# Top-k attention and a leaky-ReLU MLP on one core: eight pairs of q and k on chip, and the first two chunks' MLP work begun a step later

## The chip, the cores and the metric

The kernel runs on one core of a Trainium2 chip. The metric is device time in microseconds (us) of one execution; five executions were timed. One more was recorded by the hardware profiler, and all durations below come from that one. The engines are called by the profile's names: PE is TensorE (matrix products), DVE is VectorE, ACT is ScalarE, POOL is GpSimd, SP is SyncE, whose queue issues all DMA transfers here. Each engine, and SP's queue, works through its own list of instructions in order. The simple arrow `out<-in` in the profile names the tile written and the tiles read.

## The reference: what is computed

For 8 batches and 8 heads, with 576 tokens and a head dimension of 64, all in float32:

```python
scores = scale * np.matmul(q, k.transpose(0, 1, 3, 2))
kth = np.partition(scores, -top_k, axis=-1)[..., -top_k:-top_k + 1]   # top_k = 32
scores = np.where(scores >= kth, scores, -1000000000.0)
attn = np.exp(scores - np.max(scores, axis=-1, keepdims=True))
attn = attn / (np.sum(attn, axis=-1, keepdims=True) + 1e-09)
a = np.matmul(attn, v)
x = a.transpose(0, 2, 1, 3).reshape(4608, 512)
h = x @ w_in                                                          # 512 x 2048
out = np.maximum(0.01 * h, h) @ w_out                                 # 2048 x 512
```

The two weight matrices come as float64 words and are rounded to float32 on the chip.

## The kernel before, in words

**Weights first.** Sixteen pieces of 1 MB are loaded into `raw` tiles (three buffers, L61 and L101), and each is rounded by `round_weights` (L104 to L149) with ACT, DVE, POOL and PE. ACT and POOL read the `raw` tile; after the last piece the three `raw` buffers lie idle.

**Pairs and units.** Two heads form a pair, so a batch has four pairs and there are 32 in all. Pair p's q and k are loaded by `load_qk` (L155) into tiles `qt` and `kt` with `LOADED = 5` buffers each (L56, L60), its v by `load_v` (L162), also five. The attention works on 144 units. A whole unit is 128 query rows of one pair (both heads); a left unit is 64 rows of two pairs. An even batch has its two left units last, an odd batch has them first, so at the beginning of an odd batch all four of its pairs are needed at once (L185 to L191).

**Steps.** The main loop (L503) has one step s for each unit, written out by hand; the order of the calls is the order of the instructions on every engine. In step s:

- `top_k` of unit s runs on DVE in four parts (four calls of `slot`): one max and one min pass (L240), then MAX8 and MATCH_REPLACE8 rounds.
- `mask` of unit s-1 on POOL (L258, L259), `exponents` of it on ACT (L262), and `sums` (L267), which writes `ze`.
- `reciprocals` of unit s-2 on DVE (L271), behind the first part of `top_k(s)`: it waits for `ze`. Then `normalize` on ACT (L274).
- The normalized weights of unit s-2 are transposed: usually by `transpose` (L276), with two `split` copies on ACT (L283), two DMAs to DRAM (`apart`, L284) and a DMA transpose into `wT` (L286). For the units 3, 7, 15, 23 and 31 (`HURRIED`) it is `transpose_in_haste` on PE (L296) with two copies by ACT (L302).
- In an even step, `scores` (L193) of units s+2 and s+3: PE writes two `wide` and one `narrow` PSUM tile (L210), ACT copies them out (L217).
- `values(s)` (L491): PE multiplies `wT` by v into a `wide` PSUM tile (L323), and ACT copies the result into `x`, the input of the MLP (L337). Before step `HURRY = 20` the scores stand ahead of the values, after it behind them.
- `load_more(s)` (L464) ends the step: it loads another pair's q and k if the buffers allow, which is when the pair five places earlier has had its last scores.

**The MLP** works on chunks of tokens: two of 128, then 17 of 256 (L53). A chunk is ready when the values of its last units are there (`attended`): chunk 0 in step 5, chunk 1 in step 9, chunk 2 in step 17. Its work is a generator that yields after each small piece with that piece's cost in PE columns (`mlp`, and `hidden_of_few` for the first two chunks, `EARLY = 2`). `mlp_steps(budget)` takes pieces while the budget owed is positive; it is called seven times in each step: five times among the parts of the step above, and twice behind `values`, at its end. Until chunk 2 is ready the budget of a call is 530, later it is the backlog spread over the calls until the next chunk (`slot_budget`). When nothing is ready, what is owed is set to zero.

A piece of the first two chunks is two matmuls of 512 columns (L348 into `ph`, or L386 into `pz`) or four transposes (L358). Behind the pieces stand ACT's Prelu into `scale` (L353), ACT's copy of the transposes into `gT` (L359), and at the chunk's end ACT's copy `o_sb` (L393) and the output's DMA on SP (L394). From chunk 2 on, L374 and L380 take the place of L348 to L359. The `ph`, `pt` and `pz` tiles share two PSUM buffers.

Of the kernel before, what the change touches and what calls it, by code (L numbers as in the profile page):

```python
# [8 lines left out]
F32 = mybir.dt.float32  # L9
U32 = mybir.dt.uint32  # L10
U16 = mybir.dt.uint16
# [8 lines left out]
def kernel(  # L20
# [14 lines left out]
    NPAIR, P, S = qT.shape  # L35
# [14 lines left out]
    WCH = 1024  # L50
# [5 lines left out]
    LOADED, LOADED_V = 5, 5  # L56
# [3 lines left out]
    loads = ctx.enter_context(tc.tile_pool(name="loads", bufs=LOADED))  # L60
    raws = ctx.enter_context(tc.tile_pool(name="raws", bufs=3))  # L61
# [33 lines left out]
    def load_weights(n):  # L95
        if n >= NPIECE:
            return
        if not AS_WORDS:
            nc.sync.dma_start(piece(n), weights[n])
            return  # L100
        raw_of[n] = raws.tile([P, WCH, 4], U16, name="raw")  # L101
        nc.sync.dma_start(raw_of[n].rearrange("p n w -> p (n w)"), weights[n])
# [50 lines left out]
    qk_of, v_of = {}, {}  # L153

    def load_qk(pi):  # L155
        qt = loads.tile([P, S], F32, name="qt")
        kt = loads.tile([P, S], F32, name="kt")
        nc.sync.dma_start(qt, qT[pi])
        nc.sync.dma_start(kt, kT[pi])
        qk_of[pi] = qt, kt  # L160

    def load_v(pi):  # L162
        v_of[pi] = loads.tile([P, NKC, 2, D], F32, name="vt", bufs=LOADED_V)
        nc.sync.dma_start(v_of[pi], vk[pi])
# [54 lines left out]
    def first_scores(u):  # L219

        ps = [ps_sc.tile([P, 2, 512], F32, name="wide", bufs=2) for i in range(2)]
        for half in range(2):
            for i, pi, side, r0 in u.parts:
                qt, kt = qk_of[pi]
                d = slice(side * D, (side + 1) * D)
                nc.tensor.matmul(ps[i][:, half, 0:HS], qt[d, u.q0:u.q0 + P],
                                 kt[d, half * HS:(half + 1) * HS], start=True, stop=True)
        u.both = work.tile([P, 2, S], F32, name="s_sb", bufs=5)
        u.s = [u.both[:, i, :] for i in range(2)]
        for i in range(2):  # L230
            nc.scalar.copy(u.s[i].rearrange("p (h n) -> p h n", h=2), ps[i][:, :, 0:HS])
# [107 lines left out]
    EARLY = 2  # L339
# [22 lines left out]
    def mlp(ch):  # L362

        n = CHUNKS[ch]
        t0 = sum(CHUNKS[:ch])
        x = x_of[ch]
        if ch < EARLY:
            yield from hidden_of_few(x)
        for f0 in range(0, NFC if ch >= EARLY else 0, 2):
            ph = ps_ml.tile([P, 2, CHMAX], F32, name="ph", tag="ml")  # L370
            for i in range(2):
                f = f0 + i
                for c in range(HP):
                    nc.tensor.matmul(  # L374
                        ph[:, i, 0:n], w_in[c][:, f * P:(f + 1) * P], x[c][:, 0:n],
                        start=(c == 0), stop=(c == HP - 1),
                    )
                    if c == 1 or i == 0 and c == HP - 1:
                        yield 2 * max(n, 225)
            nc.scalar.activation(gT[:, f0:f0 + 2, 0:n], ph[:, :, 0:n], AF.Prelu, alpha=SLOPE)  # L380
            yield 2 * max(n, 225)
        for r0 in range(0, n, P):
            m = min(P, n - r0)
            pz = ps_ml.tile([P, 512], F32, name="pz", tag="ml")
            for f in range(NFC):
                nc.tensor.matmul(  # L386
                    pz[0:m, 0:DMODEL], gT[:, f, r0:r0 + m], w_out[f // 4][:, f % 4, :],
                    start=(f == 0), stop=(f == NFC - 1),
                )
                if f % 2 and f + 1 < NFC:  # L390
                    yield 2 * DMODEL
            o_sb = work.tile([P, DMODEL], F32, name="o_sb", bufs=1)
            nc.scalar.copy(o_sb[0:m], pz[0:m, 0:DMODEL])  # L393
            nc.sync.dma_start(out[t0 + r0:t0 + r0 + m, :], o_sb[0:m])  # L394
            yield 2 * DMODEL
# [10 lines left out]
    def mlp_steps(budget):  # L406
        owed[0] += budget
        while owed[0] > 0:
            if running[0] is None:
                if not ready:  # L410
                    owed[0] = 0.0
                    return
                running[0] = mlp(ready.pop(0))
            cost = next(running[0], None)
            if cost is None:
                running[0] = None
            else:
                owed[0] -= cost
                backlog[0] -= cost
# [2 lines left out]

    LAG = 3
    HURRY = 20
    HURRIED = {3, 7, 15, 23, 31}

    def values_at(n):

        return n + LAG + (n + LAG) % 2 - ((n | 1) in HURRIED)

# [13 lines left out]
    def attended(s):  # L444
        for at, ch in ready_at:
            if at == s:
                ready.append(ch)
                backlog[0] += mlp_cost(ch)

    def slot_budget(s):  # L450

        after = [at for at, _ in ready_at if at >= s]
        until = after[0] if after else s
        if len(after) >= len(CHUNKS) - EARLY:
            return EARLY_SHARE
        return backlog[0] / ((until + 1 - s) * SLOTS)
# [4 lines left out]
    with tc.manual_schedule():  # L461
        last = {p: n for n, u in enumerate(steps) for p in u.pairs}

        def load_more(s):  # L464

            for of, load, n, lag in ((qk_of, load_qk, LOADED, -2), (v_of, load_v, LOADED_V, LAG + 1)):
                while len(of) < NPAIR and (len(of) < n or last[len(of) - n] + lag <= s):
                    load(len(of))


        for n in range(3):
            load_weights(n)
        rounding = {}
        for n in range(NPIECE + 2):
            for i in (n, n - 1, n - 2) if AS_WORDS else ():
                if 0 <= i < NPIECE:
                    if i == n:
                        rounding[i] = round_weights(i)
                    next(rounding[i], None)
            load_weights(n + 3)  # L480
            if 6 <= n < 6 + HP:
                load_qk(n - 6)
            elif n == NPIECE - 3:
                first_scores(steps[0])
            elif n == NPIECE:
                first_scores(steps[1])
            if n == NPIECE - 1:
                load_v(0)
                load_v(1)

        def values(s):  # L491
            due = [u for n, u in enumerate(steps) if values_at(n) == s]
            if due:
                po = ps_sc.tile([P, 2, 512], F32, name="wide", bufs=2)[:, 0, 0:2 * P]
                po = po.rearrange("p (u n) -> p u n", u=2)
            else:
                return
            for part in (weigh_values, keep_values):
                for n, u in enumerate(due):
                    part(u, po[:, n, :])  # L500
            attended(s)

        for s in range(len(steps) + LAG + 1):  # L503
            cur, old, older, new = unit(s), unit(s - 1), unit(s - 2), ()
            if s % 2 == 0:
                new = [u for u in steps[s + 2:s + 4] if u]
            picks = top_k(cur) if cur else iter(())
            budget = slot_budget(s)

            def slot():  # L510
                next(picks, None)

            slot()
            if old:
                mask(old, 0)
                mask(old, 1)
            if older:
                reciprocals(older)
                normalize(older, 0)
                normalize(older, 1)  # L520
            mlp_steps(budget)
            slot()
            if s - 2 in HURRIED:
                transpose_in_haste(older)
            mlp_steps(budget)
            if old:
                exponents(old, 0)
            if older:
                keep_transposed(older) if s - 2 in HURRIED else transpose(older)
            slot()  # L530
            mlp_steps(budget)
            mlp_steps(budget)
            slot()
            mlp_steps(budget)
            if old:
                exponents(old, 1)
                sums(old)
            if new and s < HURRY:
                scores(new)
            values(s)  # L540
            if new and s >= HURRY:
                scores(new)
            budget = slot_budget(s + 1)
            mlp_steps(budget)
            mlp_steps(budget)
            load_more(s)
        mlp_steps(1e9)

# [57 lines left out]
```

## Time and profile before

| | |
|---|---|
| five timed executions, median | 1491.41 us (1488.08 to 1496.42) |
| the profiled execution's own time | 1491.77 us |
| its span, first to last instruction | 1490.0 us |
| mean granted clock of PE | 0.979 of full |
| longest waits of PE between 100 and 250 us | 15.0 us for ACT's score copies, 13.0 us for k |
| first matmul of chunk 2 (L374) | 242.72 us |
| DVE's start of step 17 | 225.74 us |

In the profile's groups a line gives the source line, the engine, the operation, the tile written and read, the shape, the count, the busy time and the mean of one; in an order of time, the start, the length, the instruction, and in brackets how long the engine was idle before it and what ended that wait. Each 512-column float32 matmul of the program stands as two records in the order of time.

### The profile page before, as it was taken

What the parts mean: (1) busy time and instruction counts of PE and PEld (TensorE: products, weight loads), DVE (VectorE), ACT (ScalarE), POOL (GpSimd) and SP (SyncE); (2) the same over time, 40 slices, a digit from 0 to 9 for tenths busy, and PEclk for the clock granted to TensorE, in tenths of its full rate; (3) what the DMA queues carried; (4) which work ended last, traced back from release to release, by engine and by line L of the source; (5) the groups of instructions that cost most, each with busy time, mean ns of one, the idle gap of its engine ahead of it and who ended that gap; (6) DMA issues with size and microseconds to landing.
All of it is one profiled execution on the core that took longest, in us unless ns stands there. A gap on an engine that the chain in (4) does not pass through costs nothing.

```text
span 1490.0 us, 24127 instructions
## 1 busy us (share of the span) xinstructions
PE 1400.8 (94%) x8077; PEld 932.3 (63%) x8077; DVE 1328.6 (89%) x3414; ACT 1095.5 (74%) x1979; POOL 1096.0 (74%) x742
## 2 busy tenths in 40 slices
PE   6708987999999999999999999999999999999998
PEld 2305546676666766676766666767676767676674
DVE  7999998999999999999999999999999999999600
ACT  8647786777788877777777777777777777777720
POOL 2277787888788887788887887888888887788700
PEclk9968998999999999999999999999999999999999
DMA  8623354535566466555664556656755465645510
GB/s 323 252 64 85 99 166 128 164 110 148 153 168 160 137 161 173 169 136 159 174 176 126 137 165 174 165 142 151 182 161 144 129 169 147 169 128 142 144 46 14
DMA packets 386172, 221.12 MB, mean 148 GB/s; under 512 B 331520, under 2 KB 331520, under 8 KB 384000
## 3 DMA queue, kind: packets, MB, share of 16 engines
q1 hardware_dynamic: 386048, 219.59, 53.0%
q8 instruction: 63, 1.03, 0.3%
q14 instruction: 61, 0.50, 0.1%
HBM read 46.14 MB, written 91.42 MB: 92 GB/s over the span
## 4 chain that ended last, share of the span: by engine, by line
PE 84%; DVE 6%; ACT 4%; DMA 4%; issue 1%; SPq 0%; POOL 0%; DVEq 0%; ACTq 0%
PE pz L386 34%; PE ph L374 28%; PE wide L323 11%; PE wide L210 6%; PE narrow L210 3%; DMA wT<-apart 2%; ACT split L283 2%; DMA apart<-split 1%; DVE tops L245 1%; ACT s_sb L274 1%; DVE pairs L248 1%; ACT s_sb L262 1%; PE ph L348 1%; DVE w_out L149 1%; DVE w_in L149 1%
## 5 line engine op out<-in xcount | busy, mean ns | idle before, releaser
L258 POOL TENSOR_SCALAR pen<-s_sb,tops 128x576 f32<-128x576 f32 x288 | 637.4, 2213 | 224.6 <-DVE tops L245 136.6
L245 DVE MAX8 tops<-pairs 128x8 f32<-128x288 f32 (+1 forms) x1152 | 636.0, 591 | 0.0
L386 PE MATMUL pz<-w_out,gT 128*128 128x512 f32 x1152 | 508.3, 596 | 1.4 <-ACT gT L359 1.4
L374 PE MATMUL ph<-x,w_in 128*128 128x256 f32 x2176 | 481.1, 381 | 0.0
L248 DVE MATCH_REPLACE8 pairs<-tops,pairs 128x288 f32<-128x288 f32 (+1 forms) x864 | 460.2, 538 | 0.0
L374 PEld LDWEIGHTS ph<-x,w_in 128*128 128x128 f32 x2176 | 410.7, 190 | 77.1 <-issue 22.9
L259 POOL TENSOR_TENSOR s_sb<-s_sb,pen 128x576 f32<-128x576 f32 x288 | 406.2, 1410 | 24.1
L386 PEld LDWEIGHTS pz<-w_out,gT 128*128 128x128 f32 x1152 | 215.3, 190 | 266.1 <-issue 263.4
L283 ACT COPY split<-s_sb 128x1152 uint16<-128x1152 uint16 x278 | 304.8, 1145 | 0.0
L262 ACT ACTIVATE s_sb<-s_sb,nbias 128x576 f32<-128x576 f32 x288 | 221.1, 768 | 12.4 <-POOL s_sb L259 12.4
L274 ACT ACTIVATE s_sb<-s_sb,rz 128x576 f32<-128x576 f32 x288 | 207.1, 770 | 25.6 <-DVE rz L271 25.6
L240 DVE TENSOR_TENSOR pairs<-s_sb 128x576 f32<-128x576 f32 x288 | 213.4, 779 | 9.9
L323 PEld LDWEIGHTS wide<-wT,vt 128*64 128x64 f32 x3200 | 162.6, 140 | 65.9 <-issue 18.5
L323 PE MATMUL wide<-wT,vt 128*64 128x128 f32 (+1 forms) x3200 | 181.3, 270 | 23.2 <-ACT s_sb L217 15.0
L210 PE MATMUL wide<-kt,qt 64*128 64x352 f32 (+1 forms) x632 | 118.4, 488 | 27.2 <-ACT s_sb L217 22.0
L337 ACT COPY x<-wide 128x128 f32<-128x128 f32 (+1 forms) x160 | 32.2, 261 | 151.4 <-PE wide L323 151.4
L380 ACT ACTIVATE gT<-ph 128x512 f32<-128x512 f32 x136 | 80.6, 593 | 78.9 <-PE ph L374 78.9
L217 ACT COPY s_sb<-wide 128x704 f32<-128x704 f32 x142 | 107.1, 754 | 21.7 <-PE wide L210 21.7
L210 PE MATMUL narrow<-kt,qt 64*128 64x224 f32 (+1 forms) x632 | 69.9, 359 | 8.5 <-DMA kt<-in_kT_dram 8.5
L210 PEld LDWEIGHTS wide<-kt,qt 64*128 64x128 f32 (+1 forms) x632 | 48.8, 178 | 44.4 <-ACT s_sb L217 22.5
L271 DVE RECIPROCAL rz<-ze 128x2 f32<-128x2 f32 x144 | 22.4, 156 | 59.9 <-ACT ze L267 59.8
L217 ACT COPY s_sb<-narrow 128x448 f32<-128x448 f32 x142 | 68.6, 536 | 6.8 <-PE narrow L210 6.1
(58 smaller groups left out, 550.3 us busy)
## 6 DMA issues: line engine op xcount, KB each, us to landing
apart<-split SPq DMA_DIRECT2D x278, 288.0 KB, 2.1
raw<-in_weights_dram SPq DMA_DIRECT2D x16, 1024.0 KB, 6.3
vt<-in_vk_dram SPq DMA_DIRECT2D x32, 320.0 KB, 3.4
qt<-in_qT_dram SPq DMA_DIRECT2D x32, 288.0 KB, 3.5
kt<-in_kT_dram SPq DMA_DIRECT2D x32, 288.0 KB, 4.0
out_dram<-o_sb SPq DMA_DIRECT2D x36, 256.0 KB, 2.0
wT<-apart SPq DMA_TRANSPOSE x139, 4.6
```

The lines of the kernel that those rows point to most:

```text
L210: nc.tensor.matmul(to[r0:r0 + u.rows, i, :], qt[d, u.q0:u.q0 + u.rows], kt[d, k0:k1], start=True, stop=True)
L240: nc.vector.tensor_tensor(pairs[:, :, n, :], u.both[:, :, 0:HS], u.both[:, :, HS:S], op)
L245: nc.vector.max(out=u.tops[:, i, r, :], in_=rest[i])
L248: nc.vector.match_replace(out=rest[i], in_to_replace=u.tops[:, i, r, :], in_values=rest[i], imm_value=LOWEST)
L258: nc.gpsimd.tensor_scalar(pen, u.s[i], u.tops[:, i, ROUNDS - 1, 7:8], MASKED, ALU.is_lt, ALU.mult)
L259: nc.gpsimd.tensor_tensor(u.s[i], u.s[i], pen, ALU.add)
L262: nc.scalar.activation(u.s[i], u.s[i], AF.Exp, bias=u.nbias[:, i:i + 1], scale=SCALE, accum_out=u.z[:, i:i + 1])
L274: nc.scalar.activation(u.s[i], u.s[i], AF.Copy, bias=0.0, scale=u.rz[:, i:i + 1])
L283: nc.scalar.copy(split, pairs[:, :, h])
L323: nc.tensor.matmul(po[side * D:(side + 1) * D, o, :], vt[:, c, side, :], u.wT[:, c + side * NKC if c + 1 < NKC else c, r:r + n], start=(c ...
L374: nc.tensor.matmul(ph[:, i, 0:n], w_in[c][:, f * P:(f + 1) * P], x[c][:, 0:n], start=(c == 0), stop=(c == HP - 1),)
L386: nc.tensor.matmul(pz[0:m, 0:DMODEL], gT[:, f, r0:r0 + m], w_out[f // 4][:, f % 4, :], start=(f == 0), stop=(f == NFC - 1),)
```

## The change

`load_qk` uses eight places in turn for the pairs. Five are the tiles of before; the pairs 5 to 7 of every eight go into `raw` tiles, with q in the first 576 words of a partition and k in the next 576. `load_more` therefore keeps eight pairs instead of five. The first call of it, at the end of step 0, now loads pairs 4 to 7 where it loaded pair 4; these loads stand ahead of those of v for pairs 2 to 4. `HURRIED` becomes a tuple, and in the steps 5 and 9, which end with the last values of chunks 0 and 1, the two calls of `mlp_steps` behind the values are left out. The budget of the other calls stays as it was.

```diff
     def load_qk(pi):
-        qt = loads.tile([P, S], F32, name="qt")
-        kt = loads.tile([P, S], F32, name="kt")
+        if pi % (LOADED + 3) < LOADED:
+            qt = loads.tile([P, S], F32, name="qt")
+            kt = loads.tile([P, S], F32, name="kt")
+        else:
+            raw = raws.tile([P, WCH, 4], U16, name="raw").rearrange("p n w -> p (n w)").bitcast(F32)
+            qt, kt = raw[:, 0:S], raw[:, S:2 * S]
         nc.sync.dma_start(qt, qT[pi])
         nc.sync.dma_start(kt, kT[pi])
         qk_of[pi] = qt, kt
...
-    HURRIED = {3, 7, 15, 23, 31}
+    HURRIED = (3, 7, 15, 23, 31)
...
-            for of, load, n, lag in ((qk_of, load_qk, LOADED, -2), (v_of, load_v, LOADED_V, LAG + 1)):
+            for of, load, n, lag in ((qk_of, load_qk, LOADED + 3, -2), (v_of, load_v, LOADED_V, LAG + 1)):
                 while len(of) < NPAIR and (len(of) < n or last[len(of) - n] + lag <= s):
                     load(len(of))
...
-            budget = slot_budget(s + 1)
-            mlp_steps(budget)
-            mlp_steps(budget)
+            if s - 2 not in HURRIED[:EARLY]:
+                budget = slot_budget(s + 1)
+                mlp_steps(budget)
+                mlp_steps(budget)
             load_more(s)
```

## The prediction

> **What bounds the kernel now.** I read the page first, then the waits and the busy windows by stage, then the order of time on TensorE (PE), ScalarE (ACT) and the DMA queue (SP) around the last long wait. The page's share of busy time and its chain by engine:
>
> ```profile
> PE 1400.8 (94%) x8077; PEld 932.3 (63%) x8077; DVE 1328.6 (89%) x3414; ACT 1095.5 (74%) x1979; POOL 1096.0 (74%) x742
> ...
> PE 84%; DVE 6%; ACT 4%; DMA 4%; issue 1%; SPq 0%; POOL 0%; DVEq 0%; ACTq 0%
> ```
>
> PE holds the end, but not everywhere. What PE waited for between 100 and 250 us, and then after 250:
>
> ```profile
> PE wide L323 <- ACT s_sb L217: 15.0, 2, 14.1
> PE narrow L210 <- DMA kt<-in_kT_dram: 8.5, 2, 8.3
> PE wide L210 <- DMA kt<-in_kT_dram: 4.5, 1, 4.5
> ```
>
> ```profile
> PE wide L323 <- DMA wT<-apart: 6.3, 6, 1.5
> ```
>
> All waits for k (13.0 us) lie before 250; the three other boundaries where a batch begins with its left rows show none. From 242.7 to 1490.0 PE is busy 1237.3 of 1247.3 us (busy windows). So from the first matmul of chunk 2 PE is the wall, and whatever moves that matmul moves the end by as much; before it VectorE (DVE) paces, one unit in 8.87 us. Busy time of PE, its weight loads, DVE, ACT and POOL, then granted clock, DMA share and GB/s, in the stretch that matters:
>
> ```profile
> 210.00:220.00 10.00, 5.48 (x56) 3.17 (x52) 9.90 (x30) 7.02 (x14) 8.62 (x6) 0.93 0.72 201
> 220.00:230.00 10.00, 2.45 (x14) 0.71 (x8) 9.97 (x29) 6.01 (x10) 8.50 (x7) 0.50 0.75 205
> 230.00:240.00 10.00, 7.22 (x61) 5.34 (x61) 7.59 (x19) 4.91 (x10) 8.61 (x6) 0.71 0.53 153
> ```
>
> DVE works on while PE stands, so the 13 us are not simply on the path. PE, SP and ACT in order of time show what is:
>
> ```profile
> 213.93 0.81 PE L210 MATMUL wide<-kt,qt 64*64 64x352 f32 x4
> 219.26 0.85 PE L210 MATMUL wide<-kt,qt 64*64 64x352 f32 x2 [4.52 <-DMA kt<-in_kT_dram]
> ...
> 230.95 0.64 PE L210 MATMUL narrow<-kt,qt 64*64 64x224 f32 x2 [8.35 <-DMA kt<-in_kT_dram]
> ...
> 233.07 3.68 PE L323 MATMUL wide<-wT,vt 128*64 128x128 f32 x40
> ...
> 240.38 2.40 PE L323 MATMUL wide<-wT,vt 128*64 128x128 f32 x40 [0.99 <-ACT wT L302]
> 242.72 7.17 PE L374 MATMUL ph<-x,w_in 128*128 128x256 f32 x32
> ```
>
> ```profile
> 223.00 2.34 SPq L286 DMA_TRANSPOSE wT<-apart  x1
> ```
>
> ```profile
> 225.41 0.73 ACT L217 COPY s_sb<-wide 128x704 f32<-128x704 f32 x1
> 232.00 0.97 ACT L217 COPY s_sb<-narrow 128x448 f32<-128x448 f32 x2 [5.87 <-PE narrow L210]
> ...
> 236.80 0.43 ACT L337 COPY x<-wide 128x128 f32<-128x128 f32 x2 [2.88 <-PE wide L323]
> 237.12 1.45 ACT L274 ACTIVATE s_sb<-s_sb,rz 128x576 f32<-128x576 f32 x2
> ```
>
> Step 16's scores (units 18, 19: all four pairs of batch 1) wait for pairs 5 to 7, whose buffers came free only with steps 14 and 15. ACT, in order, stands behind them, then behind step 16's values, and normalizes unit 15 at 237.12, though DVE had its reciprocal at 228.75. Unit 15's transpose, its values and chunk 2 follow: 237.12 to 242.72, 5.60 us.
>
> **Part one, eight pairs.** Three pairs more are on chip from the start; every later load stands at the step where one stood, three pairs ahead, behind the same release. Added ahead of the first three late v loads: six DMAs of 288 KB. SP issues one in about 0.45 us; the last waits until piece 15's raw buffer has been read (ScalarE's last read of one begins at 62.2). v 2 to 4 then issue near 65 instead of 54 to 56 us, and land 3.4 later. First use of v 2 is at 122.74, and SP's next instruction is at 93.5: nothing. If that cover were gone, some 10 us of delay of v would show there. The instructions of step 17 and later are in the same order on PE, ACT and SP as before.
>
> **Part two, no pieces behind values 5 and 9.** Each of the two steps drops two calls of 530; a matmul counts 512, so 2120 units are four matmuls of 0.90 us (x8 records in 3.60 to 3.70 us are four), 3.7 us of PE. Nothing is removed: all that follows comes two calls later after step 5 and four after step 9, and chunk 1 ends in step 15's third call and not behind step 14's values. I followed the new order through the rows, step by step (calling ze the sum that DVE's reciprocal waits for; in the profile DVE waits 9.3 us for it from 65 to 250, in four places):
> - Step 6: the Prelu that waited 3.19 us for its matmuls no longer stands ahead of unit 4's normalizing (1.43), and the next one (0.49) leaves too. ze of unit 5 comes near 135.0 instead of 136.9, DVE's wait of 2.49 becomes 0.7: **1.8 gained**.
> - Step 8: the first pz pieces now need the buffer of a gT copy that stands behind two splits (near 150.4). With 1.8 for the piece, 2.1 for scores, 2.4 for values, the values end near 156.8 (156.1 before); four pz matmuls (3.6) still precede unit 7's transpose; ze of unit 8 comes near 163.5, where DVE, now earlier, wants it at 161.7: **1.9 given back**.
> - Step 10: six pz matmuls (5.4) and the output copy stand ahead of ze of unit 9: near 174.3, DVE waits 2.0 instead of 2.81: **0.8 gained**.
> - Step 13: a Prelu has moved between unit 11's normalizing and the exponents; its four matmuls follow step 12's values (end 193.4) and are done at 197.0: ze at 202.4, **1.3 lost**. Step 15: three pieces and the output copy ahead of ze of unit 14: **1.2 lost**.
> Sum: step 17 starts near 227.2 on DVE, 1.5 later than its 225.74. These five are differences of one to three microseconds between long chains; their bounds are all DVE waits of steps 5 to 12 gone (2.49 + 2.81 = 5.3 earlier) and every lost item without the gains (4.4 later).
>
> **The sum at chunk 2.** Chunk 1's pz starts near 201.0, behind a gT copy; ten matmuls (9.0), scores (2.1), values (2.3) and the last six (5.4) end near 219.8. PE does step 16's scores at once, 2.1 us, to 221.9: pairs 4 to 7 have long been there. ACT reaches their copies at 226.8 (225.4 before) and needs 2.2, to 229.0. Late next are step 16's values: their PSUM buffer comes free with the first copy, 227.5, and unit 13's transposed weights land near 226.2 (split ends at 219.1, 2.1 for the copy to DRAM since the loads that stretched it to 4.09 come earlier, transpose 4.6). PE has then stood for 5.6 us; I take 3.68 for these values, as at 233.07 after the wait of 8.35, and not the 2.40 of 240.38. They end at 231.2, the x copies at 231.6; DVE's reciprocal is there at 227.2 + 3.0 = 230.2. So unit 15 is normalized at 231.6 instead of 237.1, and chunk 2 starts 5.5 us earlier, at 237.2. Without part two the same links give 231.7: its 1.5 us are covered by the transpose and the values, and cost up to 1.5 if those come sooner. Against the execution's own 1491.77 us (span 1490.0; the median of the runs is 1491.41): 1491.8 - 5.5 = **1486.3**.
>
> On the clock the row speaks first: granted 0.50 in 220 to 230, with a value group at 3.68 instead of 2.40. The Trainium skill ("TensorE: Matmul & The Clock Gate", Part 1: The HAM clock gate) says that TensorE falls to half rate after an idle window of about 3.4 us and needs about as long a busy one to come back. By it even the shorter stand of the new order still costs the 1.3 us; on a warm clock the sum would be 1485.0. By the same rule, taking matmuls from behind the values would cost if PE then stood for a window; at 126.9 the next six matmuls follow at once.
>
> **Rivals.**
> - *More goes than the wait.* If the early chains leave DVE all of its 5.3 us, step 17 starts at 220.4, the reciprocal is there at 223.5 and chunk 2 begins at 229.1: 13.6 earlier, 1478. For it: DVE is 99% busy wherever it isn't waiting for ze. Against: the values of step 16 need a transpose of 4.6 us that no part touches. Half of it, 1482, is what I count it with. Chance 0.17.
> - *The stall was hidden.* If unit 13's transpose or ACT's copies hold step 16's values until near 235, little is gained: 1489 to 1492. For it: DVE is 99.7% busy in 220 to 230, and loses only 3.84 us for it later. This is also the case that the change does nothing. Chance 0.13.
> - *Slower: a load holds SP.* Nine later pairs (13 to 15, 21 to 23, 29 to 31) go into raw buffers that hold q and k together; SP is in order, and the next unit's copies and transpose stand behind them. There is little to spare: at 265.97 PE begins values whose second transpose was issued at 261.41 and lands 4.6 later. If each such load is held longer than now, PE waits for wT once more: at the longest wait of today, 1.5 us, nine of them cost 13.5, less 5.5 gained: 1499.8. It decides from 1.1 us each. Against: the release is the scores of the step just recorded, as it was for the loads that stood there. Chance 0.10.
>
> **How the numbers follow.** The forecast case, 3 to 7.5 us gained, has 0.60. A measurement of this kernel can tell about 0.3%, 4.5 us: faster is below 1486.9. The forecast lies just past that line, so I split its 0.60 into 0.33 faster and 0.27 the same. Faster: 0.33 + 0.17 = 0.50; same: 0.27 + 0.13 = 0.40; slower 0.10. The range runs from 1480 (most of the first rival) to 1493 (the second, and part two's loss uncovered); the likeliest case's own is 1484 to 1489.
>
> **What would show it.** Right: no PE wait on a DMA of k or raw in 200 to 250; L374's first matmul near 237; the output of chunk 1 between the transposes of two steps; DVE's waits for ze at more places, each below 2.5; PE idle after 242 still near 10 us. Wrong: chunk 2 at 241 or later with values waiting for wT (second rival); waits for wT grown at the loads of step 31 and later (third); v late at 122; or chunk 2 earlier and the end not, which would mean that PE is not the wall.

## The result, and the profile after

The changed kernel takes **1492.51 us** (median of 39 executions, 1488.13 to 1495.60) against 1490.12 us for the kernel before (65 executions): a ratio of **1.0014, 95% interval 1.0010 to 1.0019**. It is 2.4 us slower, less than the 0.3% that the prediction took for no change, and on the other side of the forecast of 1486.3. The profiled execution took 1491.94 us with a span of 1490.2; that of before, at 1491.77, was one of its slower ones, so the two traces are 0.2 us apart and the medians 2.4. In the changed kernel all lines from 160 on stand four lower: L323 of before is L327, L374 is L378, L271 is L275.

The wait for k is gone, and the chain by engine has hardly moved:

```profile
PE 85%; DVE 6%; ACT 4%; DMA 3%; issue 1%; POOL 0%; DVEq 0%; SPq 0%; ACTq 0%
```

What PE waited for between 100 and 250 us, and then after 250, in the changed kernel (us in total, times, the longest):

```profile
PE wide L327 <- ACT s_sb L221: 20.3, 3, 13.5
PE pz L390 <- ACT gT L363: 5.4, 2, 2.7
PE wide L327 <- DMA wT<-apart: 3.8, 1, 3.8
```

```profile
PE wide L327 <- DMA wT<-apart: 3.9, 5, 1.6
```

13.0 us of waits for k have gone. In the kernel before, the wait for gT was small:

```profile
PE pz L386 <- ACT gT L359: 1.4, 2, 1.1
```

Three things have come: 5.3 us more behind ACT's score copies, 4.0 us more behind ACT's gT copies, and 3.8 us behind a transpose. PE in order of time shows where they stand:

```profile
201.88 11.76 PE L390 MATMUL pz<-w_out,gT 128*128 128x512 f32 x20 [2.68 <-ACT gT L363]
...
218.00 5.42 PE L390 MATMUL pz<-w_out,gT 128*128 128x512 f32 x12
...
231.26 4.25 PE L327 MATMUL wide<-wT,vt 128*64 128x128 f32 x40 [5.74 <-ACT s_sb L221]
236.72 1.43 PE L300 MATMUL wide<-ident,s_sb 128*128 128x128 f32 x9 [1.21 <-ACT s_sb L278]
241.91 4.04 PE L327 MATMUL wide<-wT,vt 128*64 128x128 f32 x40 [3.77 <-DMA wT<-apart]
245.89 7.17 PE L378 MATMUL ph<-x,w_in 128*128 128x256 f32 x32
```

Chunk 2 starts at 245.89, 3.2 us later than before and 8.7 later than forecast. DVE's waits for ze, and its start of step 17 (L244), in the changed kernel:

```profile
164.70 0.17 DVE L275 RECIPROCAL rz<-ze 128x2 f32<-128x2 f32 x1 [3.67 <-ACT ze L271]
...
175.33 0.17 DVE L275 RECIPROCAL rz<-ze 128x2 f32<-128x2 f32 x1 [1.68 <-ACT ze L271]
...
203.34 0.17 DVE L275 RECIPROCAL rz<-ze 128x2 f32<-128x2 f32 x1 [1.32 <-ACT ze L271]
...
225.08 0.17 DVE L275 RECIPROCAL rz<-ze 128x2 f32<-128x2 f32 x1 [3.91 <-ACT ze L271]
230.94 1.52 DVE L244 TENSOR_TENSOR pairs<-s_sb 128x576 f32<-128x576 f32 x2
```

These are steps 10, 11, 14 and 16. Step 17 starts at 230.94, 5.2 us later than before. And SP's queue around steps 15 and 16, start and length of each issue:

```profile
221.71 2.05 SPq L288 DMA_DIRECT2D apart<-split  x2
225.71 2.16 SPq L290 DMA_TRANSPOSE wT<-apart  x1
...
228.54 0.42 SPq L162 DMA_DIRECT2D qt<-in_qT_dram  x1
...
230.49 0.91 SPq L288 DMA_DIRECT2D apart<-split  x2
237.09 2.66 SPq L290 DMA_TRANSPOSE wT<-apart  x1
```

Unit 13's transpose follows its copies by 4.0 us, unit 14's by 6.6: the four q and k loads of step 15 (228.54 to 230.4) stand right ahead of unit 14's copies on SP and move their bytes at the same time.

### The profile page after: what moved, and what is told of

Same layout as the page of the kernel before. It is cut to its first block, busy times and chain, and to the rows that moved or that the text cites. A ratio compares the mean times of both kernels' runs of the same rounds, so it can differ in the third digit from the quotient of the medians.

```text
span 1490.2 us, 24113 instructions
## 1 busy us (share of the span) xinstructions
PE 1402.8 (94%) x8077; PEld 933.4 (63%) x8077; DVE 1328.6 (89%) x3414; ACT 1094.9 (73%) x1979; POOL 1095.9 (74%) x742
## 4 chain that ended last, share of the span: by engine, by line
PE 85%; DVE 6%; ACT 4%; DMA 3%; issue 1%; POOL 0%; DVEq 0%; SPq 0%; ACTq 0%
PE pz L390 34%; PE ph L378 29%; PE wide L327 12%; PE wide L214 6%; PE narrow L214 3%; DMA wT<-apart 2%; ACT split L287 2%; DVE tops L249 1%; ACT s_sb L266 1%; PE ph L352 1%; DVE pairs L252 1%; ACT s_sb L278 1%; DMA apart<-split 1%; DVE w_out L149 1%; DVE w_in L149 1%
## 5 line engine op out<-in xcount | busy, mean ns | idle before, releaser
L378 PE MATMUL ph<-x,w_in 128*128 128x256 f32 x2176 | 481.1, 381 | 0.0
L378 PEld LDWEIGHTS ph<-x,w_in 128*128 128x128 f32 x2176 | 410.7, 190 | 77.1 <-issue 22.9
L244 DVE TENSOR_TENSOR pairs<-s_sb 128x576 f32<-128x576 f32 x288 | 213.4, 779 | 9.9
L327 PE MATMUL wide<-wT,vt 128*64 128x128 f32 (+1 forms) x3200 | 182.9, 271 | 29.0 <-ACT s_sb L221 20.3
L327 PEld LDWEIGHTS wide<-wT,vt 128*64 128x64 f32 x3200 | 164.8, 141 | 70.9 <-ACT s_sb L221 23.6
L214 PE MATMUL wide<-kt,qt 64*128 64x352 f32 (+1 forms) x392 | 74.8, 491 | 22.7 <-ACT s_sb L221 22.0
L275 DVE RECIPROCAL rz<-ze 128x2 f32<-128x2 f32 x144 | 22.4, 156 | 60.2 <-ACT ze L271 59.9
L397 ACT COPY o_sb<-pz 128x512 f32<-128x512 f32 x36 | 21.1, 585 | 59.8 <-PE pz L390 59.8
L252 DVE MATCH_VALUE_LOAD pairs<-tops,pairs 128x8 f32 x864 | 62.9, 73 | 0.0
```

The source lines that it names most:

```text
L214: nc.tensor.matmul(to[r0:r0 + u.rows, i, :], qt[d, u.q0:u.q0 + u.rows], kt[d, k0:k1], start=True, stop=True)
L244: nc.vector.tensor_tensor(pairs[:, :, n, :], u.both[:, :, 0:HS], u.both[:, :, HS:S], op)
L252: nc.vector.match_replace(out=rest[i], in_to_replace=u.tops[:, i, r, :], in_values=rest[i], imm_value=LOWEST)
L327: nc.tensor.matmul(po[side * D:(side + 1) * D, o, :], vt[:, c, side, :], u.wT[:, c + side * NKC if c + 1 < NKC else c, r:r + n], start=(c ...
L378: nc.tensor.matmul(ph[:, i, 0:n], w_in[c][:, f * P:(f + 1) * P], x[c][:, 0:n], start=(c == 0), stop=(c == HP - 1),)
```

## The experiments

**The theory after the result.** Part one removes PE's wait for k, but the transpose of unit 14 is late next, and it is late because of the very loads that part one leaves at steps 14 and 15. Part two makes ACT and PE wait for each other, and DVE's step 17 comes later. **Rivals:** the raw buffers or the added early loads cost by themselves; or chunk 2's start doesn't set the end.

All medians of e1 to e11 against the kernel before on the same chip (1489.6, 1489.8 and 1489.3 us in the three groups of runs); the row of the change is the result above. "Chunk 2" is the start of its first matmul, "wT later" PE's waits for transposes after 250 us, "rest" the span less chunk 2, each from the run's one profiled execution.

| run | ratio, 95% interval | chunk 2 | wT later | rest |
|---|---|---|---|---|
| before | 1 | 242.72 | 6.3 | 1247.3 |
| the change | 1.0014 (1.0010 to 1.0019) | 245.89 | 3.9 | 1244.3 |
| e1: part one alone | 0.9994 (0.9983 to 1.0005) | 244.81 | 4.8 | 1245.8 |
| e2: part two alone | 1.0019 (1.0009 to 1.0029) | 244.35 | 6.5 | 1249.4 |
| **e3: part one, loads ten steps later** | **0.9949 (0.9936 to 0.9961)** | 237.01 | 3.1 | 1243.8 |
| e4: both parts, loads ten steps later | 0.9975 (0.9966 to 0.9985) | 241.88 | 3.3 | 1244.1 |
| e5: as e4, only step 5 left out | 0.9987 (0.9978 to 0.9995) | 242.56 | 4.3 | 1244.7 |
| e6: as e4, only step 9 left out | 0.9957 (0.9944 to 0.9969) | 238.72 | 3.6 | 1243.7 |
| e7: part one, loads four steps later | 1.0006 (0.9994 to 1.0018) | 237.77 | 8.7 | 1249.3 |
| e8: part one, all loads behind the transpose | 1.0287 (1.0273 to 1.0300) | 239.03 | 7.7 | 1291.2 |
| e9: part one, q and k loads behind the transpose | 1.0024 (1.0016 to 1.0033) | 237.21 | 8.3 | 1251.5 |
| e10: as e5, given back in step 6 | 0.9965 (0.9952 to 0.9977) | 237.08 | 3.1 | 1243.9 |
| e11: as e4, given back in steps 6 and 10 | 0.9961 (0.9948 to 0.9975) | 238.58 | 4.2 | 1244.9 |

**e1, part one alone.** From the changed kernel:

```diff
-            if s - 2 not in HURRIED[:EARLY]:
-                budget = slot_budget(s + 1)
-                mlp_steps(budget)
-                mlp_steps(budget)
+            budget = slot_budget(s + 1)
+            mlp_steps(budget)
+            mlp_steps(budget)
```

> Part one of the change alone: eight pairs on chip, the MLP pieces behind the values of steps 5 and 9 kept where they were. My theory (the wait for k goes, but the transpose of unit 14 is late next, because the copies that feed it share the DMA engines with the four q and k loads of step 15): no wait of PE for k or raw, step 17 of DVE starts at 225.7 as before, PE waits for wT at step 17 until about 238.4, chunk 2 starts near 242, 0.5 to 1.5 us earlier than before; total 1488.5 to 1490, 0 to 0.1% below the kernel before. Rival (part one itself costs, through the loads or the raw buffers): total 1492 to 1493, as with the whole change.

No difference that the interval tells from zero (0.9994). PE in order of time, and SP's copies and transpose of unit 14:

```profile
227.03 4.53 PE L327 MATMUL wide<-wT,vt 128*64 128x128 f32 x40 [10.84 <-ACT s_sb L221]
232.78 2.18 PE L300 MATMUL wide<-ident,s_sb 128*128 128x128 f32 x9 [1.21 <-ACT s_sb L278]
240.35 4.54 PE L327 MATMUL wide<-wT,vt 128*64 128x128 f32 x40 [5.39 <-DMA wT<-apart]
```

```profile
228.66 0.86 SPq L288 DMA_DIRECT2D apart<-split  x2
234.80 2.54 SPq L290 DMA_TRANSPOSE wT<-apart  x1
```

The same two rows in the kernel before:

```profile
227.48 0.85 SPq L284 DMA_DIRECT2D apart<-split  x2
233.78 2.59 SPq L286 DMA_TRANSPOSE wT<-apart  x1
```

Step 16's values begin 6.0 us earlier than before (227.03 against 233.07), and all of it is lost two rows later: the last values of chunk 2 need unit 14's weights, and PE waits 5.39 us for them. DVE's step 17 is at 225.82, as before (225.74). Part one is neutral by itself, as far as these executions tell, and what takes the place of the wait for k is a wait for a transpose. Chunk 2 came at 244.8, later than I expected, since the copies took longer (6.1 us from copy to transpose) and PE's granted clock was 0.50 for both value groups.

**e2, part two alone**, on the kernel before: the same four lines the other way round, and the tuple.

> Part two alone: five pairs as before, no MLP pieces behind the values of steps 5 and 9. My theory (the moved pieces make ACT and PE wait for each other, and ze comes late for DVE): step 17 of DVE starts near 231 instead of 225.7; PE still waits for k at step 16, until about 234; chunk 2 starts at 245 to 248; total 1492.5 to 1495. Rival (part two is neutral and part one costs): step 17 near 226, total 1490, no difference from the kernel before.

Slower by 0.19%. DVE's step 17 starts at 230.25, and chunk 2 at 244.35, a little earlier than I had it. So the loss of the whole change is part two's; the rival that part two is neutral is out.

**e3 and e4, the loads ten steps later.** In `load_more`, on e1 and on the changed kernel:

```diff
-            for of, load, n, lag in ((qk_of, load_qk, LOADED + 3, -2), (v_of, load_v, LOADED_V, LAG + 1)):
+            for of, load, n, lag in ((qk_of, load_qk, LOADED + 3, 8), (v_of, load_v, LOADED_V, LAG + 1)):
```

> Part one alone, and each later pair's q and k are loaded ten steps later (the lag of the loads is 8 instead of -2), so that no q or k load stands in steps 14 and 15. My theory: the copies of units 13 and 14 to DRAM land in 2.1 us again, PE has no wait for wT or k between 200 and 250, chunk 2 starts near 236, 6 to 7 us earlier than before, and the end moves with it: 1483 to 1485. Rival (chunk 2's start is held by something else, such as the PSUM buffer or DVE): chunk 2 at 241 or later and 1489 to 1491. Second rival (PE after chunk 2 isn't the wall): chunk 2 near 236 and the total still above 1489.

1482.43 us, 0.51% faster than before: the lowest ratio of this study, though e6's interval overlaps with it. SP around unit 14, and PE:

```profile
221.29 1.38 SPq L288 DMA_DIRECT2D apart<-split  x2
224.66 2.34 SPq L290 DMA_TRANSPOSE wT<-apart  x1
```

```profile
224.01 4.53 PE L327 MATMUL wide<-wT,vt 128*64 128x128 f32 x40 [9.96 <-ACT s_sb L221]
229.75 2.18 PE L300 MATMUL wide<-ident,s_sb 128*128 128x128 f32 x9 [1.21 <-ACT s_sb L278]
232.82 4.26 PE L327 MATMUL wide<-wT,vt 128*64 128x128 f32 x40 [0.89 <-ACT wT L306]
237.01 7.17 PE L378 MATMUL ph<-x,w_in 128*128 128x256 f32 x32
```

The transpose follows its copies by 3.4 us instead of 6.1, the wait for wT is gone, and chunk 2 starts 5.7 us earlier than before. About 2 us of that were there before step 16: its DVE starts that step at 214.89 against 216.94. Of these, 0.9 us stood at 69 us already; the rest came with PE's clock, granted in full from 117.2 to 120.6 us here and by half in before. It isn't this execution alone: with no q or k load in steps 14 and 15, chunk 2 starts at 237.1 to 238.7 in e6, e7, e10 and e11 too. The end moved by 9.2 in the traces and 7.2 in the medians. The raw buffers carry q and k here as in the change, and PE shows no wait for them.

> The whole change, and the later pairs' q and k loaded ten steps later as well. My theory: step 17 of DVE stays near 231, since no load makes that; only the wait for wT at step 17 (3.77 us) goes: chunk 2 at 241.5 to 242.5, total 1488 to 1490, 5 us behind part one alone with late loads. Rival (the loads cause all of the loss): step 17 near 226 and a total as low as that of part one with late loads.

1486.41, 4.0 us behind e3. DVE's step 17 at 231.39 and chunk 2 at 241.88 are as expected; the total is some 2 us better than that. It fits that PE also waits less for transposes later on (3.3 against 6.3 us).

**e5 and e6, which of the two places.** On e4, the condition `s - 2 not in HURRIED[:EARLY]` becomes `s != 5` and `s != 9`.

> Eight pairs with the loads ten steps later, and the MLP calls left out behind the values of step 5 only (not of step 9). It is to tell which of the two left-out places makes ze late. My theory: the Prelu's wait in step 6 goes and DVE's wait at step 7 with it, but at step 10 DVE waits 3 to 4 us for ze, as with both; the waits at steps 14 and 16 come from a delay of four calls and are smaller with two. Total about half way, 1483.5 to 1485.5. Rival (step 5 alone carries the loss): 1486 to 1487. Second rival (step 9 alone does): 1482 to 1483.

> The same with the calls left out behind the values of step 9 only. My theory: DVE's wait of 2.5 at step 7 is back, the one at step 10 isn't there, those at steps 14 and 16 come in part; total half way again, 1483.5 to 1485.5. If step 5 alone carries the loss: 1482 to 1483; if step 9 alone does: 1486 to 1487.

My halves were wrong: step 5 carries the loss (0.9987, chunk 2 at 242.56; 1487.89 us is even above the rival's 1486 to 1487), step 9 costs nothing that these runs tell (0.9957 against e3's 0.9949). In e5 DVE waits for ze at steps 10, 11, 14 and 16, as in the change, and at 12. The first pz matmuls of chunk 0, in e5 and then in e10 (below), where the order is shifted back:

```profile
149.93 3.64 PE L390 MATMUL pz<-w_out,gT 128*128 128x512 f32 x4 [2.68 <-ACT gT L363]
```

```profile
146.86 3.70 PE L390 MATMUL pz<-w_out,gT 128*128 128x512 f32 x8 [1.15 <-ACT gT L363]
```

Two matmuls of the program (x4) take as long in e5 as four (x8) in e10: behind this wait of 2.68 us PE's granted clock is 0.50, behind that of 1.15 it is 1.00.

**e7, the loads at steps 18 and 19** (lag 2 on e1).

> Part one alone, and the later loads four steps later than in the change (lag 2) instead of ten: they now stand in steps 18 and 19, where PE begins values the moment the transpose lands. My theory (loads stretch the copies to DRAM of whatever unit is being transposed, wherever they stand): chunk 2 near 237 as with ten steps, but PE waits for wT between 250 and 300 by 2 to 5 us, which it didn't; total 1484 to 1487. Rival (only the place at steps 14 and 15 is bad): no new wait, 1482 to 1483.

1490.24: all of e3's gain is gone, though chunk 2 starts at 237.77 (the profiled execution took 1488.86). PE's waits for wT after 250 are 8.7 us instead of 3.1. One of them, on SP and on PE:

```profile
261.47 0.85 SPq L288 DMA_DIRECT2D apart<-split  x2
268.89 2.72 SPq L290 DMA_TRANSPOSE wT<-apart  x1
```

```profile
283.69 1.39 PE L327 MATMUL wide<-wT,vt 128*64 128x64 f32 x40 [2.69 <-DMA wT<-apart]
```

7.4 us from copies to transpose, with four loads right ahead of them. So it isn't only the place at steps 14 and 15. In e3 the later loads stretch the copies behind them too, here to 6.7 us:

```profile
978.81 0.86 SPq L288 DMA_DIRECT2D apart<-split  x2
985.53 2.42 SPq L290 DMA_TRANSPOSE wT<-apart  x1
```

But PE has other work there, and none of e3's waits for wT after 250 is over 1.3 us. So a later place pays only where PE has room. The total of e7 is worse than I expected (1484 to 1487).

**e8 and e9, the loads behind the transpose on SP.** On e1, `load_more` of a step is called in the next one, right behind `transpose`; in e9 for q and k alone:

```diff
             if older:
                 keep_transposed(older) if s - 2 in HURRIED else transpose(older)
+            if s:
+                load_more(s - 1, [(qk_of, load_qk, LOADED + 3, -2)])
...
-            load_more(s)
+            load_more(s, [(v_of, load_v, LOADED_V, LAG + 1)])
```

> Part one alone, with the loads of each step recorded in the next step behind that step's transpose, so that on SP they follow the two copies to DRAM and the transpose instead of standing ahead of them (steps 14 and 15 still release them). My theory: the copies of units 13 and 14 land in 2 to 3 us; the loads share only with the transposes themselves; PE waits for wT at step 17 not at all or below 1.5 us; chunk 2 at 237 to 239.5, total 1482.5 to 1485.5. Rival (sharing with the transpose is as bad as with the copies): chunk 2 at 241 or later, 1488 to 1490.

e8 moved the loads of v too, which I had overlooked, and v came too late in the later batches:

```profile
PE wide L327 <- DMA vt<-in_vk_dram: 30.6, 11, 7.0
```

It tells nothing of q and k but that chunk 2, at 239.03, came as early as expected, though PE waited 3.4 us for wT at step 17 and I had expected at most 1.5.

> The run before this that put loads behind the transpose moved those of v as well, and PE then waited 30.6 us for v; here only the q and k loads are recorded one step later, behind that step's copies and transpose on SP, and v stays in its place. Part one alone otherwise. My theory (queue and DMA engines, not the number of pairs, set unit 14's transpose): chunk 2 at 238 to 240 as in the run before, where PE waited 3.4 us for wT at step 17 since the loads of step 15 still share with the copies of unit 14; no wait for v; total 1484 to 1487. Rival (the 1532 was not v): above 1500 again.

v is on time again, and chunk 2 starts at 237.21, a little earlier than expected, with 1.80 us of wait left (for ACT, not wT). But the total is 1493.24, slower than before: the loads now stand between one unit's transpose and the next unit's copies, and PE's waits for wT after 250 are 8.3 us, the longest 3.7. My total (1484 to 1487) was wrong for that: I had looked at step 16 alone.

**e10 and e11, the left-out calls given back in the next step.** On e4:

```diff
-            if s - 2 not in HURRIED[:EARLY]:
-                budget = slot_budget(s + 1)
-                mlp_steps(budget)
-                mlp_steps(budget)
+            budget = slot_budget(s + 1)
+            for i in range({5: 0, 6: 4}.get(s, 2)):
+                mlp_steps(budget)
```

and `{5: 0, 6: 4, 9: 0, 10: 4}` in e11.

> Eight pairs, loads ten steps later, and the two MLP calls behind the values of step 5 left out but made up by four calls instead of two at the end of step 6, so that the order from step 7 on is that of the kernel before. My theory (the loss of part two is not the empty place in step 5 but the shift of all that follows, which puts the first pz matmuls behind a gT copy in step 8): DVE's wait at step 7 is 0 to 0.7, none at step 10, 2.8 at step 11 as without part two; total 1480.5 to 1482.5, no slower than part one with late loads. Rival (leaving step 5 out is what costs): DVE waits 3 us or more at step 10, total 1486 to 1488.

1484.53, 2 us above what I expected: the loss of e5 is gone but for what the intervals can't tell from e3, and DVE has no wait at step 10. So leaving the place of step 5 empty is not what costs; the shift of all that follows is. But it gains nothing either: DVE's wait of step 7 has moved to step 8, where the pieces given back stand ahead of ze:

```profile
144.55 0.17 DVE L275 RECIPROCAL rz<-ze 128x2 f32<-128x2 f32 x1 [2.05 <-ACT ze L271]
```

> The same with the calls of step 9 left out too and made up at the end of step 10: the whole change, with the loads later and the left-out calls given back in the next step. My theory: DVE waits below 1 us at steps 7 and 11, no new wait of PE for gT; chunk 2 at 234 to 237; total 1479.5 to 1482. Rival (any shift behind step 9 costs as much as it gains): 1482 to 1484.

1484.20, outside what I expected. The wait of step 11 falls to 0.36, and one of 2.70 comes in step 12. Given back, part two moves DVE's waits by a step and saves nothing: steps 6 to 12 hold 5.4 us of them in e11 and 5.5 in e1.

## Why the prediction was wrong, point by point

Chunk 2 came 8.7 us later than forecast (245.89 against 237.2), and four terms of the chain make that up: ACT reached step 16's score copies 3.7 us later (230.48 against 226.8), held up by the same matmuls that made DVE late (second step below); step 16's values took 4.25 us and not 3.68; PE waited 3.77 us for unit 14's transpose where 1.0 stood before; and the last values took 4.04 us where the prediction kept the 2.40 of before, because the clock was at half again.

- **PE is the wall from chunk 2 on: right.** Rest less the waits for wT is 1240.1 to 1241.0 in ten of the thirteen rows, before and the change among them (1247.3 - 6.3 = 1241.0; 1244.3 - 3.9 = 1240.4). What it left out is the second term: I took the waits for wT as given, and they moved from 3.1 to 8.7 us with the place of the loads. In e2 and e9 it is 2 to 3 us more: PE's granted clock was 0.50 for 3.4 us (from 418.0) and for 6.8 us (from 908.8) there, and at no time after chunk 2's first matmuls in the ten. In e8 the waits for v are not in these two terms either.
- **The wait for k goes: right**, and so is that the early loads cost nothing: v 2 to 4 were issued at 64.3 us, the next SP instruction stood at 93.5.
- **"Late next are step 16's values": the step that failed.** Those values did begin as worked out, when ACT's first copy freed their PSUM buffer (231.26). But in e1, where nothing else changed, they came 6 us earlier, and chunk 2 still didn't. Late next was unit 14's transpose, which step 17's values need. I had followed unit 13's weights and the loads of step 14, which do come earlier for it, and not unit 14's and the loads of step 15. The rows that show it were in the trace of before (beside e1 above): 6.3 us from copies to transpose for what takes 3.2 without loads. The transpose landed 5.4 us after its issue, near 239.2, 1.2 us ahead of the values at 240.38. A gain of 5.5 had to check everything that had less than 5.5 us of room.
- **"Ten matmuls (9.0)": the second step that failed.** My own working had PE wait nearly 3 us for a gT copy before them (matmuls done at 197.0, some 1.1 us of transposes, start at 201.0), and priced them at the full clock. They took 11.76, and the two of step 8 took 3.60 instead of 1.8. That made ze of unit 14 late by 3.91 instead of 1.2 and, with 3.67 instead of 1.9 at step 10, step 17 late by 5.2 instead of 1.5. The other waits came as worked out (step 7: none, against 0.7; step 11: 1.68 against 2.0; step 14: 1.32 against 1.3). The five terms of the prediction for step 17 add up to 1.8 us lost, not the 1.5 that it says; that changes little.
- **The 1.5 us of part two were to be covered.** Against a step 17 that late they aren't: e4 is 4 us behind e3.
- **The rivals.** What happened is nearest to the second (the stall was hidden): a transpose holds chunk 2, with part two's loss on top. But the rival named unit 13's transpose and step 16's values, and it was unit 14's and step 17's. The slower rival's mechanism, loads into raw buffers that hold SP, didn't show: PE never waited for raw, and e3 uses the same buffers.
- The prediction weighed the clock at step 16 and behind the values of step 5, and not at the gT copies. The Trainium skill ("TensorE: Matmul & The Clock Gate", Part 1: The HAM clock gate) names an idle window of about 3.4 us for the fall to half rate. Here stands of 2.68 us were enough behind the gT copies, and one of 2.69 us elsewhere was not; the clock rows are below, and the measurement decides.

Not settled: why PE waits 2.4 us less for transposes after 250 in the changed kernel's trace than in that of before (3.9 against 6.3), with loads at the same steps. Each is one execution, and e1 and e2 lie at 4.8 and 6.5.

## What to carry to other kernels

When a wait is to go, list everything that has less room behind it than the gain, with the transfers first: here PE no longer waited for the loads, but they stayed in the DMA queue, ahead of the copies that fed the next transpose. Buffers that allow an early load pay only if the load also moves to where nothing that is nearly late shares the queue with it; ten steps later was worth 7 us, four steps later nothing. Work pieces deferred by a constant budget shift everything behind them, so check the stretch where the shift ends, and price PE by the clock it will have there.

## What the runs showed of the hardware that I had not expected

**A stand of 2.68 us was enough to halve PE's clock for 6.8 us, though not everywhere.** Stretches of 1 us in the changed kernel (busy us of PE, its weight loads, DVE, ACT and POOL, then granted clock, DMA share and GB/s):

```profile
199.00:200.00 1.00, 0.20 (x2) 0.00 (x0) 1.00 (x2) 1.00 (x3) 1.00 (x1) 1.00 0.00 0
200.00:201.00 1.00, 0.00 (x0) 0.00 (x0) 1.00 (x3) 1.00 (x2) 0.92 (x2) 0.97 0.00 0
201.00:202.00 1.00, 0.12 (x1) 0.12 (x1) 1.00 (x5) 1.00 (x3) 1.00 (x1) 0.50 0.76 295
...
207.00:208.00 1.00, 1.00 (x3) 0.43 (x2) 1.00 (x4) 1.00 (x2) 0.00 (x0) 0.61 0.62 184
208.00:209.00 1.00, 1.00 (x4) 0.47 (x3) 1.00 (x2) 0.81 (x3) 0.30 (x1) 1.00 0.75 288
```

PE stopped at 199.2, behind eight short transposes, and began again at 201.88. The clock fell at about 200.9, 1.7 us after the last matmul, and rose near 207.8, after 5.9 us of dense work. All seven waits of 2.67 or 2.68 us for a gT copy, in the change, e2, e4 and e5, brought such a fall. Waits of 1.15 us, as in e6 and e10, left the clock at full. But e7's wait of 2.69 us, between two groups of values (shown above), left it at full too:

```profile
283.00:284.00 1.00, 0.31 (x10) 0.34 (x12) 1.00 (x5) 0.00 (x0) 0.95 (x1) 1.00 0.85 291
284.00:285.00 1.00, 1.00 (x37) 0.94 (x33) 1.00 (x4) 0.00 (x0) 1.00 (x1) 1.00 1.05 404
```

And one of 1.73 us at 416.56 in e2 was followed by 0.50 from 418.0 to 421.4. So the length of a stand doesn't decide alone. The stretches at half rate between 100 and 1470 us last 3.41 us or a multiple of it in all thirteen traces, so the place of a stand in time may count, and so may the transposes ahead of it; no run separates them.

**Loads right ahead of a copy to DRAM stretch it.** From the issue of a unit's two copies to that of its transpose it takes 3.2 to 3.7 us in nine of ten cases with no load near (before, 100 units with none issued in the 8 us ahead). With four q and k loads (1.15 MB) issued right ahead it takes 5.5 to 7.4 at the five places read above (unit 14's in before, the change, e1 and e9, and a later one in e7), and 5.0 to 6.7 at the three such places of e3. Whether it is the order of the queue or the share of the DMA engines that stretches it, no run separates.
